# A decode block on one core: the last gate's weights carried by the last cache transfer, and one block of w2 brought in 26 five-row transfers

## Chip, core and metric

The kernel runs on one core of one Trainium2 chip. The metric is the device time of one execution in microseconds (us); lower is better. Before the change it is 1056.6 us, the median of three runs (1055.8 to 1057.46).

## What is computed

One token passes through an attention block with a long cache and then through a feed-forward block, both with modulated layer norms. All data is float32. Cut to what matters:

```
mod = silu(c) @ w_mod                 # c: 1 x 640, w_mod: 640 x 3840
sa, ca, ga, sb, cb, gb = six parts of mod, 640 each
h = layernorm(x) * (1 + ca) + sa
q = h @ wq                            # 32 heads of 192
o = softmax(q k^T / sqrt(192)) v      # k and v caches: 32 heads x 8192 x 192
x = x + ga * (o @ wo)                 # wo: 6144 x 640
h = layernorm(x) * (1 + cb) + sb
f = relu(h @ w1 + b1) ** 2            # w1: 640 x 1536
x = x + gb * (f @ w2 + b2)            # w2: 1536 x 640
```

The caches hold 403 MB, so nearly all of the work is bringing data in once.

## The kernel before

The data comes in as **transfers of about 8 MB** on one queue, that of SyncE (SP). They land in a ring of three slots, each 64.5 KB on every one of the 128 partitions (`slot`, L96; `load`, L197). `plan` (L50) cuts the caches into 53 chunks. A chunk holds some key positions, some units of values (eight positions each) and, in some chunks, a piece of wq ("q") or of wo ("o") at the end of each row ("mixed" transfers). Chunk 50 has the last keys, chunks 51 and 52 only values (nine and seven units), chunk 51 also the wo piece of pair 14. Chunk 52 comes in two pieces, of four and three units. After the chunks come three loads for the end, each into the next free slot: wm1 (the wo piece of the last pair 15 and the parts ga, sb, cb of w_mod), w1 (gb's part of w_mod, then w1 itself), and w2. They are cut at `WM_CUT`, `W1_CUT` and `W2_CUT` (L43 to L45), so that reading can begin before all has landed. wm1's first piece has the wo piece and the first three of five row blocks of the modulation weights. Load n+3 is issued by `load(n + 3)` at the end of step n (L401) and waits until chunk n has been read.

In the loop over chunks (L354 to L401) the values go to TensorE (`values`, L298, sums over positions with the softmax weights as stationary operand), the keys to VectorE (`multiply`, L249, by the query, and `scores`, L257, which sums over 192), with a part of the first addition on GpSimd (L376). `softmax` (L268) turns a head's scores into weights, `evict` (L303) brings a finished head back from PSUM and transposes it, `turn` (L318) scales it, `attend` (L324) multiplies a pair of heads by wo into `att_a`.

The order of work is written out by hand, and every engine works through its own instructions in that order. The order of the end on TensorE is: values of chunk 51, `attend(14)`, values of chunk 52, the transpose of the last evicted head, `attend(15)` (needs wm1's first piece), `mod(2, 3)` (L171; the three parts ga, sb, cb; its last two row blocks need wm1's second piece) with `gather` (L338) after the third of five row blocks, the two small sums of `layernorm` (L137), `gate(5)` (L183 to L192: twenty matmuls with gb's weights from w1's first piece, then four copies on ScalarE), the matmuls `pf` with w1 (L428), one idle matmul (L438), and the matmuls `py` with w2 (L446). `pf` needs `hT2`, the transposed result of the second layer norm (L422). Between `pf` and `py` VectorE makes `fT` (L431 to L434).

Two tiles that the change touches are held for the whole program: `qb` (L224), a ring of query rows that `query` fills and `multiply` reads, and `att_s` (L235), which is zeroed on VectorE early in the program and used only by `gather`.

Of the kernel before, what the change touches and what calls it, by code (L numbers as in the profile page):

```python
# [35 lines left out]
SRING = 4 * NPOS  # L36
WQ = KB * QC
UNIT = E * DH
SLOT = 84 * DH
VPC = 5  # L40
LEAD_FROM = 1300
LEAD = 120
W1_CUT = (KB * D + 3 * FF, KB * D + KB * FF)  # L43
W2_CUT = (8 * D, 11 * D, 12 * D)
WM_CUT = (WO + 9 * D, WO + 15 * D)  # L45
WARM = 1
EPS = 1e-5
# [2 lines left out]
def plan():  # L50

    chunks, kp, vp, q, o = [], 0, 0, 1, 0
    while kp < H * NPOS or vp < H * NPOS // E:
        room, w = SLOT, []
        if o < NPAIR - 1 and 2 * (o + 1) * NPOS // E <= vp:
            w.append(("o", o))
            o, room = o + 1, room - WO
        used = (QC * (q - 2) - 1) // DH + 1 if q > 2 else 0
        if q < NQ and kp >= NPOS * (QC * q // DH) - 3 * NPOS // 2 and kp >= NPOS * used:
            w.append(("q", q))  # L60
            q, room = q + 1, room - WQ
        if not chunks:
            nk, nv = NPOS, 0
        else:
            v = VPC - 1 if kp >= LEAD_FROM else VPC
            nk = min(H * NPOS - kp, (room - v * UNIT) // DH)
            if kp + nk - E * (vp + v) > LEAD:
                v += 1
                nk = min(H * NPOS - kp, (room - v * UNIT) // DH)
            nv = min(H * NPOS // E - vp, (room - nk * DH) // UNIT)  # L70
            while nv and ((vp + nv - 1) // (NPOS // E) + 1) * NPOS > kp + nk:
                nv -= 1
            nk = min(H * NPOS - kp, (room - nv * UNIT) // DH)
        chunks.append((kp, nk, vp, nv, w))
        kp, vp = kp + nk, vp + nv
    assert q == NQ and o == NPAIR - 1
    return chunks


def width(chunk):  # L80
    return chunk[1] * DH + chunk[3] * UNIT + sum(WO if t == "o" else WQ for t, _ in chunk[4])


PLAN = plan()


@with_exitstack
def block_kernel(ctx: ExitStack, tc: tile.TileContext, kv, wm0, wm1, w1, w2, out):
    nc = tc.nc
    const = ctx.enter_context(tc.tile_pool(name="const", bufs=1))  # L90
    strm = ctx.enter_context(tc.tile_pool(name="strm", bufs=3))
# [100 lines left out]
            nc.scalar.activation(mods[r, m], ps[r, DG * (g % 2):DG * (g % 2 + 1)], AF.Copy)  # L192

    chunk_t = {}
    start = [sum(width(c) for c in PLAN[:n]) * P for n in range(len(PLAN))]

    def load(n):  # L197
        if n < len(PLAN):
            chunk_t[n] = slot(f"chunk{n}")
            m = width(PLAN[n])  # L200
            cuts = (m,) if n + 1 < len(PLAN) else ((PLAN[n][3] + 1) // 2 * UNIT, m)
            pieces = [(kv[start[n]:start[n] + P * m].rearrange("(p n) -> p n", p=P), cuts)]
        else:
            name, src, cuts = (("wm1_t", wm1, WM_CUT), ("w1_t", w1, W1_CUT), ("w2_t", w2, W2_CUT))[n - len(PLAN)]
            chunk_t[name] = slot(name)
            n, pieces = name, [(src, cuts)]
        for src, cuts in pieces:
            a = 0
            for b in cuts:
                nc.sync.dma_start(chunk_t[n][:, a:b], src[:, a:b])  # L210
                a = b
# [9 lines left out]
        return ca1  # L221

    h1 = layernorm(x_c, 1, scale_a, lambda: ma[:, :KB, 0], "ln1")
    qb = const.tile([P, RING], F32, name="qb")  # L224

    def query(u, w):
        w = w.rearrange("p (b n) -> p b n", b=KB)
        ps = psum.tile([P, 512], F32, tag="q", name=f"ps_q{u}", bufs=2)
        for b in range(KB):
            nc.tensor.matmul(ps, h1[:, b:b + 1].to_broadcast([P, P]), w[:, b], start=(b == 0), stop=(b == KB - 1))  # L230
        nc.scalar.activation(qb[:, QC * u % RING:QC * u % RING + QC], ps, AF.Copy, scale=DH ** -0.5)  # L231


    att_a = psum.tile([P, 512], F32, tag="att", name="att_a")
    att_s = const.tile([P, D], F32, name="att_s")  # L235
    nc.vector.memset(att_s, 0.0)
    query(0, wm0_t[:, KB * 2 * D:KB * 2 * D + WQ])

    sc = const.tile([P, SRING], F32, name="sc")
# [63 lines left out]
    def evict(h):  # L303

        n = 32 * NV
        if h % 2 == 0:
            os_t["part"] = work.tile([P, 2, ED], F32, tag="os", name=f"os{h // 2}")
        os_ = os_t["part"]
        om = work.tile([P, ED, E], F32, tag="om", name=f"om{h}", bufs=1)
        nc.vector.tensor_mul(om[:n], ps_t.pop(h)[:n].rearrange("p (d e) -> p d e", e=E),  # L310
                             mask[:n, None, :].to_broadcast([n, ED, E]))
        nc.vector.tensor_reduce(os_[:n, h % 2], om[:n], axis=AX.X, op=ALU.add)  # L312
        if h % 2:
            i = h // 2
            os_t[i] = psum.tile([P, 512], F32, tag="sm", name=f"ps_oT{i}", bufs=2)
            nc.tensor.transpose(os_t[i][:, :n], os_[:n].rearrange("p a d -> p (a d)"), ident[:n, :n])  # L316

    def turn(i):  # L318
        oT = work.tile([P, NV], F32, tag="oT", name=f"oT{i}")
        nc.vector.tensor_reduce(oT, os_t[i][:, :96].rearrange("p (j r) -> p j r", j=NV), axis=AX.X, op=ALU.add)  # L320
        nc.vector.tensor_scalar(oT, oT, ri_t.pop(i), None, op0=ALU.mult)  # L321
        os_t[i] = oT
# [14 lines left out]

    def gather():  # L338

        nc.vector.tensor_copy(att_s[96:, :512], att_a[96:, :512])  # L340
        for j in range(NV):
            r = slice(32 * j, 32 * (j + 1))
            nc.scalar.activation(att_s[r, 512:], att_a[r, (D - 512) * j:(D - 512) * (j + 1)], AF.Copy)
        att_t.append(psum.tile([P, 512], F32, tag="o", name="att", bufs=3))
        for g in range(G):
            nc.tensor.matmul(att_t[0][32 * g:32 * (g + 1), :DG], sel.to_broadcast([P, 32]),
                             att_s[:, DG * g:DG * (g + 1)], start=True, stop=True)
# [6 lines left out]
    for n, (kp, nk, vp, nv, extra) in enumerate(PLAN):  # L354
        t = chunk_t.pop(n)
        kt = t[:, :nk * DH].rearrange("p (i d) -> p i d", d=DH) if nk else None
        vt = t[:, nk * DH:nk * DH + nv * UNIT].rearrange("p (j g n) -> p j g n", g=NV, n=E * ED) if nv else None
        at = nk * DH + nv * UNIT
        wo_t = None
        for what, k in extra:  # L360
            w = t[:, at:at + (WO if what == "o" else WQ)]
            at += w.shape[1]
            if what == "q":
                query(k, w)
            else:
                wo_t = (k, w)
        done = (kp + nk) // NPOS - 1 if nk and (kp + nk) // NPOS > kp // NPOS else None
        late = [v for v in range(vp, vp + nv) if v // (NPOS // E) not in p_t]
        for v in range(vp, vp + nv):
            if v not in late:  # L370
                values(vt[:, v - vp], v)
        if nk:
            multiply(kt, kp, nk)
            m = nk - POOL * nk // 16
            half = kt[:, m:, :DH // 2]
            nc.gpsimd.tensor_add(half, half, kt[:, m:, DH // 2:])  # L376
        if to_invert is not None:
            inverse(to_invert)
            to_invert = None
        evicted, to_evict = to_evict, []  # L380
        for h in evicted:
            evict(h)
        if nk:
            scores(kt[:, :m], kp)
        for h in evicted:
            if h % 2:
                turn(h // 2)
        if nk:
            scores(half, kp + m)
        if done is not None:  # L390
            softmax(done)
            if done % 2:
                to_invert = done // 2
        for v in late:
            values(vt[:, v - vp], v)
        for v in range(vp, vp + nv):
            if v % (NPOS // E) == NPOS // E - 1:
                to_evict.append(v // (NPOS // E))
        if wo_t is not None:
            attend(*wo_t)  # L400
        load(n + 3)  # L401

    wm1_t, w1_t, w2_t = chunk_t["wm1_t"], chunk_t["w1_t"], chunk_t["w2_t"]
    gb_t = w1_t[:, :KB * D].rearrange("p (b n) -> p b n", b=KB)
    w1_t = w1_t[:, KB * D:KB * (FF + D)].rearrange("p (b n) -> p b n", b=KB)
    w2_t = w2_t[:, :FB * D].rearrange("p (b n) -> p b n", b=FB)

    for h in to_evict:
        evict(h)
    turn(NPAIR - 1)  # L410
    attend(NPAIR - 1, wm1_t[:, :WO])
    mod(2, 3, wm1_t[:, WO:WO + KB * 3 * D].rearrange("p (b n) -> p b n", b=KB), gather)
# [8 lines left out]

    hT2 = columns(layernorm(x1, 32, scale_b, lambda: mods[:, 3], "ln2"), DG, "hT2")  # L422

    gate(5, gb_t)
    pf = psum.tile([P, 512], F32, tag="q", name="ps_f", bufs=2)
    for b in range(KB):
        for g in range(G):
# [15 lines left out]
    py = psum.tile([P, 512], F32, tag="q", name="ps_y", bufs=2)  # L443
    for b in range(FB):
        for g in range(G):
            nc.tensor.matmul(py[32 * g:32 * (g + 1), :DG], fT[:, b], w2_t[:, b, DG * g:DG * (g + 1)],  # L446
                             start=(b == 0), stop=(b == FB - 1))
    y = const.tile([P, DG], F32, name="y")
    nc.vector.tensor_mul(y, py[:, :DG], mods[:, 5])
# [44 lines left out]
```

## Time and profile before

| | |
|---|---|
| median of 3 runs | 1056.6 us |
| profiled execution, its own time | 1055.57 us |
| span of the profiled execution | 1053.8 us |
| VectorE busy | 830.2 us (79%) |
| TensorE busy | 495.8 us (47%) |
| moved by the DMA engines | 452.15 MB, 429 GB/s over the span |
| TensorE clock granted, mean | 0.713 |

A page of the profile lists busy time, transfers, the chain of work that ended last, and groups of instructions by line of the kernel (L298 is line 298). PE is TensorE, PEld its weight load, DVE VectorE, ACT ScalarE, POOL GpSimd, SP SyncE; SPq is SP's queue of transfers. Busy shares are averages over the whole span; what the end is worth is read from the timeline and the windows of the last 50 us.

### The profile page before, as it was taken

The page shows a single profiled execution, that of the slowest core. Times are in us where ns is not written, and L with a number is a line of the kernel's source. Part 1 is how long each engine was busy: PE and PEld are TensorE (multiplying, and loading weights), DVE is VectorE, ACT ScalarE, POOL GpSimd, SP SyncE. Part 2 cuts the span into 40 slices and gives each one's busy share as a digit, 9 for nine tenths or more (in the row PEclk, how much of TensorE's full clock was granted, in tenths as well). Part 3 has the DMA queues.
Part 4 walks back from the last instruction along what each step waited for, and adds up shares of the span by engine and source line. Part 5 has one row for each costly group of instructions (what it writes and reads, how often), then busy time and mean ns, then how long its engine had stood idle before and what let it go on. Part 6 is the DMA issues. An engine that isn't in the chain of part 4 may idle for free.

```text
span 1053.8 us, 5121 instructions
## 1 busy us (share of the span) xinstructions
PE 495.8 (47%) x2102; PEld 134.6 (13%) x2102; DVE 830.2 (79%) x428; ACT 43.4 (4%) x122; POOL 188.1 (18%) x57
## 2 busy tenths in 40 slices
PE   2153335455352363536344357344446346345286
PEld 1010011011010010101011011011011011011023
DVE  2898878877959969887797895999887977988822
ACT  1000000000000000000000000000000000000001
POOL 0212121121212202212121121122211211211200
PEclk9676576777675686668676577676777767768699
DMA  9999999999999999999999999999999999999997
GB/s 408 434 429 431 429 441 438 441 431 433 430 431 431 432 433 430 433 435 438 435 427 436 433 427 430 436 439 433 431 432 431 432 436 433 437 433 430 419 431 311
DMA packets 8959, 452.15 MB, mean 429 GB/s; under 512 B 996, under 2 KB 1000, under 8 KB 1256
## 3 DMA queue, kind: packets, MB, share of 16 engines
q1 hardware_dynamic: 8936, 451.83, 99.3%
q8 instruction: 16, 0.26, 0.1%
q14 instruction: 7, 0.06, 0.0%
HBM read 451.82 MB, written 0.00 MB: 429 GB/s over the span
## 4 chain that ended last, share of the span: by engine, by line
DMA 56%; DVE 31%; PE 11%; ACT 1%; issue 0%; SPq 0%; DVEq 0%
DMA chunk<-in_kv 53%; DVE chunk L249 16%; DVE sc L257 13%; PE ps_o L298 5%; DMA w_t<-in_w 2%; PE ps_q L230 2%; PE att_a L331 2%; DMA wm_t<-in_wm 1%; DVE os L312 1%; DVE om L310 1%; ACT p L281 0%; PE ps_mod L179 0%; PE ps_mx L273 0%; PE ps_mod L188 0%; PE att_a L333 0%
## 5 line engine op out<-in xcount | busy, mean ns | idle before, releaser
L249 DVE TENSOR_TENSOR chunk<-chunk,qb 128x8064 f32<-128x8064 f32 (+19 forms) x81 | 419.7, 5211 | 128.4 <-DMA chunk<-in_kv 123.2
L257 DVE TENSOR_REDUCE sc<-chunk 128x25 f32<-128x4800 f32 (+21 forms) x109 | 333.9, 3097 | 0.4
L298 PE MATMUL ps_o<-chunk,p 128*32 128x512 f32 x1536 | 296.7, 736 | 73.7 <-DMA chunk<-in_kv 64.3
L376 POOL TENSOR_TENSOR chunk<-chunk 128x1824 f32<-128x1824 f32 (+9 forms) x51 | 187.4, 3674 | 806.3 <-DVE chunk L249 548.4
L273 PE MATMUL ps_mx<-ident,mp 128*128 128x128 f32 x32 | 14.6, 455 | 343.9 <-DVE mp L271 343.9
L298 PEld LDWEIGHTS ps_o<-chunk,p 128*32 128x32 f32 x1536 | 67.4, 131 | 278.1 <-issue 188.1
L331 PE MATMUL att_a<-chunk,oT 128*32 128x512 f32 x90 | 63.4, 863 | 42.2 <-DVE oT L321 42.2
L230 PE MATMUL ps_q<-chunk,ln_h 128*128 128x512 f32 x110 | 66.9, 769 | 26.1 <-DMA chunk<-in_kv 26.1
L273 PEld LDWEIGHTS ps_mx<-ident,mp 128*128 128x128 f32 x32 | 5.6, 176 | 373.0 <-DVE mp L271 304.0
L281 ACT ACTIVATE p<-sc,nm 128x256 f32<-128x256 f32 x32 | 16.2, 507 | 649.9 <-DVE nm L275 649.9
L230 PEld LDWEIGHTS ps_q<-chunk,ln_h 128*128 128x128 f32 x110 | 26.5, 252 | 64.5 <-issue 35.1
L310 DVE TENSOR_TENSOR om<-ps_o,mask 96x512 f32<-96x512 f32 x32 | 21.6, 675 | 8.5 <-PE ps_o L298 8.5
L275 DVE TENSOR_REDUCE nm<-ps_mx 128x1 f32<-128x128 f32 x32 | 9.3, 292 | 19.5 <-PE ps_mx L273 19.5
L312 DVE TENSOR_REDUCE os<-om 96x64 f32<-96x512 f32 x32 | 21.8, 682 | 1.1
L331 PEld LDWEIGHTS att_a<-chunk,oT 128*32 128x32 f32 x90 | 11.7, 145 | 77.4 <-DVE oT L321 44.4
L320 DVE TENSOR_REDUCE oT<-ps_oT 128x3 f32<-128x96 f32 x16 | 4.0, 248 | 20.3 <-PE ps_oT L316 20.3
L286 PE MATMUL ps_sum<-ident,wide 128*128 128x128 f32 x16 | 7.5, 467 | 22.4 <-ACT wide L284 22.4
L179 PE MATMUL ps_mod<-wm_t,silu 128*32 128x320 f32 (+1 forms) x80 | 9.2, 608 | 15.5 <-DVE silu L167 15.5
L316 PE MATMUL ps_oT<-ident,os 96*128 96x96 f32 x16 | 5.0, 313 | 22.3 <-DVE os L312 22.3
L333 PE MATMUL att_a<-chunk,oW 128*96 128x384 f32 x30 | 14.1, 550 | 0.0
L231 ACT ACTIVATE qb<-ps_q 128x512 f32<-128x512 f32 x12 | 7.2, 597 | 136.7 <-PE ps_q L230 136.7
L329 ACT ACTIVATE oW<-oT 128x96 f32<-128x96 f32 x16 | 4.5, 280 | 177.5 <-DVE oT L321 177.5
(84 smaller groups left out, 100.9 us busy)
## 6 DMA issues: line engine op xcount, KB each, us to landing
chunk<-in_kv SPq DMA_DIRECT2D x38, 8064.0 KB, 37.5
chunk<-in_kv SPq DMA_DIRECT2D x11, 8000.0 KB, 38.3
chunk<-in_kv SPq DMA_DIRECT2D x2, 7872.0 KB, 38.5
chunk<-in_kv SPq DMA_DIRECT2D x1, 6144.0 KB, 27.6
wm_t<-in_wm SPq DMA_DIRECT2D x1, 4493.5 KB, 13.6
w_t<-in_w SPq DMA_DIRECT2D x1, 3904.0 KB, 20.7
wm_t<-in_wm SPq DMA_DIRECT2D x1, 3840.0 KB, 23.8
chunk<-in_kv SPq DMA_DIRECT2D x1, 3072.0 KB, 28.2
```

What stands on the lines that cost most here:

```text
L230: nc.tensor.matmul(ps, h1[:, b:b + 1].to_broadcast([P, P]), w[:, b], start=(b == 0), stop=(b == KB - 1))
L249: nc.vector.tensor_mul(pr, pr, q[:, None, :].to_broadcast([P, b - a, DH]))
L257: nc.vector.tensor_reduce(sc[:, a % SRING:a % SRING + b - a], src[:, a - first:b - first], axis=AX.X, op=ALU.add)
L273: nc.tensor.transpose(ps[:, :P], mp.to_broadcast([P, P]), ident)
L275: nc.vector.tensor_reduce(nm, ps[:, :P], axis=AX.X, op=ALU.max, negate=True)
L281: nc.scalar.activation(p, s[:, :, None].to_broadcast([P, NPOS, 32 // E]), AF.Exp, bias=nm, accum_out=sp[:, h % 2:h % 2 + 1])
L298: nc.tensor.matmul(ps_t[h][32 * g:32 * (g + 1)], p[:, E * j:E * (j + 1)].rearrange("p e r -> p (e r)"), t[:, g], start=(j == 0), stop=last)
L310: nc.vector.tensor_mul(om[:n], ps_t.pop(h)[:n].rearrange("p (d e) -> p d e", e=E), mask[:n, None, :].to_broadcast([n, ED, E]))
L312: nc.vector.tensor_reduce(os_[:n, h % 2], om[:n], axis=AX.X, op=ALU.add)
L331: nc.tensor.matmul(att_a[96:, :512], oT[:, j:j + 1].to_broadcast([P, 32]), w[:, j, :512], start=(first and j == 0), stop=(last and j == NV ...
L333: nc.tensor.matmul(att_a[:96, :NV * (D - 512)], oW.rearrange("p j r -> p (j r)"), w[:, :, 512:], start=first, stop=last)
L376: nc.gpsimd.tensor_add(half, half, kt[:, m:, DH // 2:])
```

## The change

The part of w_mod that makes gb moves from the head of the w1 load to the end of chunk 52's rows, in its second piece ("g" in the plan). `gate(5)` moves from after the second layer norm to right after the last `evict`, before `turn(15)` and `attend(15)`. Row block 0 of w2 leaves the w2 load. It gets an input array `w2x` and a tile `w2x_t` of its own, filled by 26 transfers: one after each `load(n + 3)` for n from 4 to 29, five rows of 640 floats each and three rows in the last. The w2 load keeps the other eleven blocks and is cut at new places; its last piece is now only the last 160 columns of the last block. `qb` and `att_s` now share one buffer: `att_s` is made in `gather`, and zeroed there on GpSimd.

```
+EXTRA = {"o": WO, "q": WQ, "g": KB * D}
-W1_CUT = (KB * D + 3 * FF, KB * D + KB * FF)
-W2_CUT = (8 * D, 11 * D, 12 * D)
+W1_CUT = (3 * FF, KB * FF)
+W2_CUT = (7 * D, 11 * D - DG, 11 * D)
+FEW = 5
+FEW_FROM = 4
...
+    chunks[-1][4].append(("g", 0))
...
+    w2x_t = const.tile([P, D], F32, name="w2x_t")
...
-    qb = const.tile([P, RING], F32, name="qb")
+    qb = work.tile([P, RING], F32, name="qb", tag="qb", bufs=1)
...
-    att_s = const.tile([P, D], F32, name="att_s")
-    nc.vector.memset(att_s, 0.0)
...
 def gather():
+        att_s = work.tile([P, D], F32, name="att_s", tag="qb", bufs=1)
+        nc.gpsimd.memset(att_s, 0.0)
...
         load(n + 3)
+        a = FEW * (n - FEW_FROM)
+        if 0 <= a < P:
+            b = min(a + FEW, P)
+            nc.sync.dma_start(w2x_t[a:b], w2x[a:b])
...
     for h in to_evict:
         evict(h)
+    gate(5, gb_t)
     turn(NPAIR - 1)
     attend(NPAIR - 1, wm1_t[:, :WO])
...
     hT2 = columns(layernorm(x1, 32, scale_b, lambda: mods[:, 3], "ln2"), DG, "hT2")
-    gate(5, gb_t)
     pf = psum.tile([P, 512], F32, tag="q", name="ps_f", bufs=2)
...
-            nc.tensor.matmul(py[...], fT[:, b], w2_t[:, b, ...],
+            nc.tensor.matmul(py[...], fT[:, b], (w2_t[:, b - 1] if b else w2x_t)[...],
```

Sizes: gb's weights are 1600 KB, one block of w2 is 320 KB, one row of it 2560 bytes. All bytes are still brought in once.

More of the change, by code (lines that the diff above doesn't have):

```diff
@@ L76, in plan, with block_kernel @@
     assert q == NQ and o == NPAIR - 1
+    chunks[-1][4].append(("g", 0))
     return chunks
 def width(chunk):
-    return chunk[1] * DH + chunk[3] * UNIT + sum(WO if t == "o" else WQ for t, _ in chunk[4])
+    return chunk[1] * DH + chunk[3] * UNIT + sum(EXTRA[t] for t, _ in chunk[4])
 PLAN = plan()
 @with_exitstack
-def block_kernel(ctx: ExitStack, tc: tile.TileContext, kv, wm0, wm1, w1, w2, out):
+def block_kernel(ctx: ExitStack, tc: tile.TileContext, kv, wm0, wm1, w1, w2, w2x, out):
     nc = tc.nc
@@ L358, in block_kernel @@
         at = nk * DH + nv * UNIT
-        wo_t = None
+        wo_t = gb_t = None
         for what, k in extra:
-            w = t[:, at:at + (WO if what == "o" else WQ)]
+            w = t[:, at:at + EXTRA[what]]
             at += w.shape[1]
@@ L364, in block_kernel @@
                 query(k, w)
+            elif what == "g":
+                gb_t = w.rearrange("p (b n) -> p b n", b=KB)
             else:
@@ L401, in block_kernel @@
         load(n + 3)
+        a = FEW * (n - FEW_FROM)
+        if 0 <= a < P:
+            b = min(a + FEW, P)
+            nc.sync.dma_start(w2x_t[a:b], w2x[a:b])
     wm1_t, w1_t, w2_t = chunk_t["wm1_t"], chunk_t["w1_t"], chunk_t["w2_t"]
-    gb_t = w1_t[:, :KB * D].rearrange("p (b n) -> p b n", b=KB)
-    w1_t = w1_t[:, KB * D:KB * (FF + D)].rearrange("p (b n) -> p b n", b=KB)
-    w2_t = w2_t[:, :FB * D].rearrange("p (b n) -> p b n", b=FB)
+    w1_t = w1_t[:, :KB * FF].rearrange("p (b n) -> p b n", b=KB)
+    w2_t = w2_t[:, :(FB - 1) * D].rearrange("p (b n) -> p b n", b=FB - 1)
     for h in to_evict:
         evict(h)
+    gate(5, gb_t)
     turn(NPAIR - 1)
@@ L445, in block_kernel @@
         for g in range(G):
-            nc.tensor.matmul(py[32 * g:32 * (g + 1), :DG], fT[:, b], w2_t[:, b, DG * g:DG * (g + 1)],
+            nc.tensor.matmul(py[32 * g:32 * (g + 1), :DG], fT[:, b], (w2_t[:, b - 1] if b else w2x_t)[:, DG * g:DG * (g + 1)],
                              start=(b == 0), stop=(b == FB - 1))
@@ L475 @@
     v = a(A_v_cache).reshape(H, P, NPOS // E, E, NV, ED).transpose(1, 0, 2, 4, 5, 3).reshape(P, H * NPOS // E, UNIT)
+    gb = rows(wm[:, 5 * D:], KB)[None]
     kv = [np.concatenate([k[:, kp:kp + nk].reshape(P, -1), v[:, vp:vp + nv].reshape(P, -1)]
-                         + [(wo if what == "o" else wq)[i] for what, i in extra], axis=1).reshape(-1)
+                         + [{"o": wo, "q": wq, "g": gb}[what][i] for what, i in extra], axis=1).reshape(-1)
           for kp, nk, vp, nv, extra in PLAN]
@@ L483 @@
         "wm1": np.concatenate([wo[-1], rows(wm[:, 2 * D:5 * D], KB)], axis=1),
-        "w1": np.concatenate([rows(wm[:, 5 * D:], KB), rows(B_w1, KB)], axis=1),
-        "w2": rows(B_w2, FB),
+        "w1": rows(B_w1, KB),
+        "w2": rows(B_w2, FB)[:, D:],
+        "w2x": rows(B_w2, FB)[:, :D],
     }
```

## The prediction

> **What bounds the kernel now.** I read the page first: the transfers and their rate, then the last part of the chain of waits.
>
> ```profile
> span 1053.8 us, 5121 instructions
> GB/s 408 434 429 431 429 441 438 441 431 433 430 431 431 432 433 430 433 435 438 435 427 436 433 427 430 436 439 433 431 432 431 432 436 433 437 433 430 419 431 311
> DMA packets 8959, 452.15 MB, mean 429 GB/s; under 512 B 996, under 2 KB 1000, under 8 KB 1256
> q8 instruction: 16, 0.26, 0.1%
> wm_t<-in_wm SPq DMA_DIRECT2D x1, 3840.0 KB, 23.8
> wm_t<-in_wm SPq DMA_DIRECT2D x1, 1920.0 KB, 28.1
> w_t<-in_w SPq DMA_DIRECT2D x1, 1536.0 KB, 24.0
> w_t<-in_w SPq DMA_DIRECT2D x1, 320.0 KB, 26.6
> ```
>
> Only the last slice (311 GB/s) falls away, so the transfers run back to back until a few us before the end. The change moves the same bytes, so no stage before the end gets shorter; the question is the last 50 us. Here is the chain in order of time, with columns start, us, what:
>
> ```profile
> 943.04 39.25 DMA chunk<-in_kv
> ...
> 1001.66 9.86 PE ps_o L298 x54
> ...
> 1015.98 20.69 DMA w_t<-in_w
> 1036.71 4.43 PE ps_mod L188 x20
> 1041.14 3.41 PE ps_f L428 x40
> ...
> 1046.98 3.50 PE ps_y L446 x96
> ```
>
> Chunk 50's landing, at 943.04 + 39.25 = 982.3, is the last one that the middle of the kernel waits for. The chain then names w1's first piece (landed at 1036.67) and the gate that follows it. But the page's chain follows only what came last. TensorE's timeline shows what runs beside it:
>
> ```profile
> 1015.88 6.21 PE L298 MATMUL ps_o<-chunk,p 128*32 128x512 f32 x42
> 1023.61 0.30 PE L316 MATMUL ps_oT<-ident,os 96*128 96x96 f32 x1 [1.52 <-DVE os L312]
> 1024.59 2.76 PE L331 MATMUL att_a<-wm_t,oT 128*32 128x512 f32 x6 [0.68 <-DVE oT L321]
> ...
> 1030.81 1.79 PE L179 MATMUL ps_mod<-wm_t,silu 128*32 128x480 f32 x16
> ...
> 1037.75 0.34 DVE L122 STREAM_TRANSPOSE hT<-ln_h 128x160 f32<-128x160 f32 x1
> ```
>
> From 1001.66 to the end of `mod(2, 3)` at 1032.60 TensorE has almost no gap, and the layer norm after it delivers hT2 at 1038.09, only 3.0 us before `pf` starts. So the gate can be worth 3.0 us at most, not 4.43.
>
> **The change, part by part. The gate.** It now sits between the transpose that ends at 1023.91 and `attend(15)`. How long it takes there depends on TensorE's clock, the column after POOL in the windows view (the next one is the mean DMA share):
>
> ```profile
> 1022.10:1024.60 2.50, 0.31 (x2) 0.15 (x2) 1.86 (x4) 0.03 (x1) 0.00 (x0) 1.00 1.03 439
> 1032.60:1036.40 3.80, 0.71 (x5) 0.59 (x4) 2.42 (x8) 0.06 (x1) 0.00 (x0) 1.00 0.96 410
> 1036.40:1039.81 3.41, 3.10 (x12) 1.48 (x14) 1.36 (x5) 0.20 (x1) 0.00 (x0) 0.50 1.09 458
> 1039.81:1044.40 4.59, 4.59 (x50) 1.62 (x46) 0.00 (x0) 1.18 (x4) 0.00 (x0) 1.00 0.97 410
> ```
>
> After 3.8 us in which TensorE worked 0.71 us, the clock was half for 3.41 us, and 3.10 us of the gate ran in that time. At full clock the gate is 3.10 / 2 + (1041.14 - 1039.81) = 1.55 + 1.33 = 2.9 us. At its new place the clock was 1.00, so it ends at 1023.91 + 2.9 = 1026.8. Its four ScalarE copies then stand ahead of `attend(15)`'s own copy (oW), but that is first needed 2.7 us after `attend(15)` begins, so I cost them at nothing.
>
> Behind the gate `attend(15)` waits: it needs wm1's first piece, and gb's 1600 KB now come ahead of that (1.638 MB / 429 GB/s = 3.8 us). The timeline of SP has the issue times:
>
> ```profile
> 998.97 0.81 SPq L210 DMA_DIRECT2D wm_t<-in_wm  x2
> 1015.98 7.44 SPq L210 DMA_DIRECT2D w_t<-in_w  x5
> ```
>
> The first piece lands at 998.97 + 23.8 + 3.8 = 1026.6, the second near 999.4 + 28.1 + 3.8 = 1031.3. `attend(15)` therefore starts at 1026.8 instead of 1024.59, **2.2 us later**, and everything to hT2 shifts with it: the last two blocks of `mod(2, 3)` run from 1033.0, after the second piece; hT2 is ready at 1040.3. w1's bytes end where they did, since what stands ahead of that point is the same sum: its second piece lands at 1016.4 + 24.0 = 1040.4, and `pf` needs it only for the last two of its five blocks. `pf` starts at 1040.35 instead of 1041.07: **0.7 us earlier**. Of the 4.43 us the gate gave up, 2.9 are paid again ahead of `attend(15)`.
>
> **pf's clock.** The gate was also what brought the clock back: `pf` ran at 1.00. Now TensorE is nearly idle from 1034.8 (1032.60 + 2.2) to 1040.35, 5.5 us, longer than the 4.1 us that lost the clock before. If `pf` then runs at half clock as long as the gate did (3.10 us), it gets 1.55 us longer. The bounds are 0 (the clock holds) and 3.4 us (all of `pf`'s 3.41 us at half clock); I take **+1.55**, from the nearest row. The Trainium skill, page "TensorE: Matmul & The Clock Gate", section "Part 1: The HAM clock gate (the "warmup" mystery)", says that an idle window of about 3.4 us halves the clock and about 3.4 us of work restores it; the rows above agree (3.41 us at 0.50). By its figure the term would be 1.7 us.
>
> The same clock adds a smaller term. The values of chunk 51 (9.86 us from 1001.66) began at half clock:
>
> ```profile
> 1002.27:1005.68 3.41, 3.41 (x15) 0.77 (x12) 1.19 (x2) 0.00 (x0) 0.00 (x0) 0.50 0.95 405
> ```
>
> That lasted to the end of this window, 4.0 us. The clock changes in whole steps of 3.41 us (from 1005.68 to 1036.40 are nine), and where they fall against the work is chance. 3.10 us of work in a step were enough above, so the slow stretch can last from 3.1 to 3.1 + 3.41 = 6.5 us, 4.8 in the middle. Before, up to 3.0 us of delay there was covered by the gate's wait; afterwards `attend(15)` has 0.2 us of cover. The middle length costs (4.8 - 4.0) / 2 - 0.2 = **0.2 us**, the longest 1.0.
>
> **The end of w2.** `py` follows `pf` by the same 2.4 us and so moves with it. Its last block begins 3.2 us after its start, near 1051, and w2's last piece landed near 1023.0 + 26.6 = 1049.6. A block less of w2 takes 0.75 us off that (0.328 MB / 429 GB/s), but `py` does not wait there, so the saving is worth **0**. The smaller last piece is worth nothing for the same reason.
>
> **The 26 transfers.** Their cost on an engine is read from the last rows of w2, which have the same 2560 bytes (the transfers of 1048.3 to 1049.0):
>
> ```profile
> DMA packets 27, 0.06 MB, mean 84 GB/s; under 512 B 4, under 2 KB 4, under 8 KB 27
> q1 hardware_dynamic: 27, 0.06, 21.5%
> ```
>
> 21.5% of 16 engines' 0.7 us is 2.41 us for 23 rows: 0.105 us each. A load writes a small completion packet for every engine that takes part: 62 loads x 16 + 4 = 996, the count under 512 B on the page. So the 62 loads of 128 rows used all 16 engines and the output of four rows used four; five rows will use five. The Trainium skill, page "DMA: Bandwidth & Descriptors", section "Why a DMA increments its semaphore by 16 and not by 1", says so too, and that these are always the lowest-numbered engines; the count agrees, the numbers of the engines no view here shows. If they are always the same five, each gets 26 x 0.105 = 2.7 us more. If they rotated, each of 16 would get 0.85 us, no more than the block of w2 that leaves its end.
>
> Whether 2.7 us on five engines cost anything depends on how evenly the sixteen run. The last column but one of these windows is the share of them at work:
>
> ```profile
> 1044.00:1045.00 1.00, 1.00 (x10) 0.30 (x2) 0.43 (x1) 0.00 (x0) 0.00 (x0) 1.00 0.91 376
> 1047.00:1048.00 1.00, 1.00 (x32) 1.00 (x36) 0.29 (x1) 0.00 (x0) 0.00 (x0) 1.00 0.48 197
> 1049.00:1050.00 1.00, 1.00 (x37) 1.00 (x32) 0.00 (x0) 0.00 (x0) 0.00 (x0) 1.00 0.01 3
> ```
>
> The engines finish between 1045 and about 1049, 4 us apart, and about half of them before 1047. An engine that is under 4 - 2.7 = 1.3 us behind the first has room; one at the tail makes every landing after it 2.7 us later. I take 0 and keep 2.7 as the other end. On SP an issue is 0.4 us (998.97, two in 0.81) and the loads around it are 37 us ahead of their landing, so nothing queued behind a small transfer is late.
>
> **The rest.** The zeroing of att_s cost 0.59 us on VectorE, where the first `multiply` waited 5.17 us for the query afterwards; on GpSimd it follows that engine's last addition and is needed 30 us later. Nothing either way, at most 0.6 us if it slowed the last scores.
>
> ```profile
> 24.11 0.59 DVE L236 MEMSET att_s<- 128x640 f32 x1
> ...
> 31.97 12.96 DVE L249 TENSOR_TENSOR chunk<-chunk,qb 128x12288 f32<-128x12288 f32 x1 [5.17 <-ACT qb L231]
> ```
>
> **Sum:** -0.7 + 1.55 + 0.2 = +1.05 us. The profiled execution took 1055.57 us, so it would take 1056.6; that execution is 1.0 us under the median of 1056.6, and against the median I get **1057.7 us**.
>
> **The rivals.** *The clock holds* through the 5.5 us, or returns after a moment: then -0.7 is all that is left, 1055.9 us. For it: the small sums of the layer norm run in the gap; against it: they ran in the 3.8 us above too.
>
> *The five engines are late ones.* This ends slower. Landings from chunk 50 on are 1.9 to 2.7 us later, 1059.6 to 1060.4 us. It decides as soon as one of the five is over 1.3 us behind the first. For it: half of the engines are; against it: only that the other half is not.
>
> *A small transfer costs more than its bytes.* Foreign packets do: the 16 instruction packets took 0.1% of 16 x 1053.8 us, 1.05 us each, for 16 KB that take 0.6 us at 27 GB/s. With 0.44 us more each, 26 cost 11 us more on five engines, about 1068 us. Against it: the rows of w2 above, in the loads' own queue, show no such gap.
>
> *The gate is hidden and the transfers set the end:* `pf` would start at 1038.1, and `py` would meet w2's last piece. That lands at 1049.6 - 0.75 = 1048.9, and with one of twelve blocks of `py` (0.3 us) behind it `py` ends at 1049.2 instead of 1050.48: 1.3 us less, 1055.3 us. Against it: `attend(15)` is behind the gate.
>
> **How the numbers follow.** Forecast 42%, clock holds 15%, late engines 28%, dear small transfers 8%, gate hidden 7%. 0.2% is 2.1 us, about what a measurement of this kernel can tell from no change. Slower by more: late engines, dear transfers and a tenth of the forecast, 40%. Faster by more: no case reaches it unless w2 lands earlier than I count, 5%. Within: 55%. The range runs from the clock that holds (1055.9) to the late engines with some of the clock's bound (1060.8); the dear transfers and the hidden gate stay outside. The forecast's own range is 1056.6 to 1058.7.
>
> **What would show it.** The gate at about 2.9 us with `attend(15)` right behind it near 1027; hT2 near 1040.3; a clock of 0.50 at the start of `pf`, which takes about 5 us. Were chunk 50 to land 2 us later than 982.3, late engines are the cause. A `pf` that starts before 1039.5 or `py` waiting for w2 would prove the sum wrong.

## The result and the profile after

| | before | after |
|---|---|---|
| median | 1056.37 us (6 runs, 1055.8 to 1057.46) | 1061.14 us (6 runs, 1060.45 to 1061.85) |
| ratio, 95% interval | 1 | 1.0042 [1.0032, 1.0053] |
| profiled execution | 1055.57 us | 1061.85 us |
| its span | 1053.8 us | 1060.1 us |

The change makes the kernel 4.8 us slower. The prediction said 1 us slower, and the time lies 0.3 us above its range. The page of the changed kernel first:

```profile
span 1060.1 us, 5151 instructions
GB/s 407 430 429 445 436 429 432 432 434 429 430 436 429 432 429 428 427 428 433 434 430 429 427 437 431 433 434 431 436 427 433 431 443 433 429 433 427 426 426 254
DMA packets 9216, 452.15 MB, mean 427 GB/s; under 512 B 1125, under 2 KB 1257, under 8 KB 1385
```

The bytes are the same. The packets under 512 B are 129 more than before: 128 of them are completion packets of the 26 transfers, one for each row (25 x 5 + 3), so within a transfer each row went to an engine of its own. The mean rate is 2 GB/s lower. The chain of waits, in order of time (start, us, what):

```profile
947.26 39.26 DMA chunk<-in_kv
986.54 8.56 DVE chunk L252
...
1003.20 27.61 DMA wm_t<-in_wm
```

Chunk 50 lands at 986.5 instead of 982.3: **4.2 us late**, before anything of the moved gate has run. TensorE's timeline of the end (start, us, line, what, in brackets the idle time before and what ended it):

```profile
1027.75 2.91 PE L192 MATMUL ps_mod<-chunk,silu 128*64 128x320 f32 x20
1030.95 2.73 PE L334 MATMUL att_a<-wm_t,oT 128*32 128x512 f32 x6 [0.29 <-DMA wm_t<-in_wm]
...
1037.14 1.79 PE L183 MATMUL ps_mod<-wm_t,silu 128*32 128x480 f32 x16
1044.53 6.24 PE L438 MATMUL ps_f<-w_t,hT 128*32 128x384 f32 x40 [1.89 <-issue]
1053.13 0.48 PE L456 MATMUL ps_y<-w2x_t,fT 128*32 128x160 f32 x8 [1.31 <-DVE fT L126]
```

The same matmuls `pf` before:

```profile
1041.07 3.43 PE L428 MATMUL ps_f<-w_t,hT 128*32 128x384 f32 x40
```

The gate takes 2.91 us, `attend(15)` follows it after a wait of 0.29 us for wm1's first piece, and `pf` starts 3.46 us later than the 1041.07 of before: the 4.2 us of chunk 50 less the 0.7 us that the prediction gave the gate. `pf` itself takes 6.24 us instead of 3.43, 2.8 us more. `py` waits for `fT`, not for w2. So the 6.3 us between the two spans are +4.2 (landings), -0.7 (gate) and +2.8 (`pf`); between the medians there are 4.8, since the profiled execution of before (1055.57 us) was faster than all six of its timed runs and that of after was its slowest.

The windows show the clock around `pf` (busy us of PE, PEld, DVE, ACT and POOL, then TensorE's clock, DMA share, GB/s):

```profile
1040.01:1043.43 3.42, 0.71 (x4) 0.59 (x4) 1.88 (x10) 0.26 (x1) 0.00 (x0) 1.00 1.03 433
1043.43:1046.84 3.41, 2.31 (x16) 0.90 (x20) 0.93 (x3) 0.00 (x0) 0.00 (x0) 0.50 0.97 411
1046.84:1050.25 3.41, 3.41 (x25) 1.12 (x20) 0.00 (x0) 0.00 (x0) 0.00 (x0) 0.50 0.71 293
```

As before the change, a stretch in which TensorE worked 0.71 us is followed by half clock. But `pf` began 1.1 us into the next step, worked 2.31 us of it, and did not get the clock back at its end; a second step at half clock followed, up to 1050.25.

Where do the 4.2 us come from? Windows over long stretches in the middle, of before and then of after:

```profile
200.00:400.00 200.00, 92.14 (x363) 24.15 (x362) 161.46 (x75) 7.05 (x21) 35.13 (x10) 0.71 1.00 433
400.00:600.00 200.00, 91.01 (x345) 23.45 (x345) 164.64 (x81) 6.57 (x20) 39.79 (x11) 0.67 1.00 433
700.00:900.00 200.00, 96.67 (x370) 26.17 (x368) 168.77 (x79) 7.68 (x23) 40.33 (x11) 0.72 1.00 433
```

```profile
200.00:400.00 200.00, 90.58 (x362) 23.72 (x362) 160.52 (x75) 7.06 (x21) 35.12 (x10) 0.72 1.00 431
400.00:600.00 200.00, 89.38 (x344) 23.12 (x344) 162.06 (x78) 6.57 (x20) 39.79 (x11) 0.69 1.00 430
700.00:900.00 200.00, 99.47 (x373) 26.37 (x371) 168.05 (x75) 7.69 (x23) 36.62 (x10) 0.72 1.00 433
```

The small transfers are issued after chunks 4 to 29, so they run from about 160 to 640 us. In the two windows that lie within it the rate is 2 to 3 GB/s lower although the DMA share is 1.00 as before; after 700 us it is 433 again. 2.5 of 433 GB/s over these 400 us are 2.3 us. A few more rows on five engines would not lower the rate of all of them together, so something else is lost there. On SP nothing waits for a small transfer:

```profile
169.37 0.34 SPq L215 DMA_DIRECT2D chunk<-in_kv  x1
169.75 0.32 SPq L412 DMA_DIRECT2D w2x_t<-in_w2x  x1
```

The packet records of the trace tell the two losses apart. Every engine writes its completion packet when its share of a load is done, so each load has sixteen such times. The first and the last of them, in us, and their distance (the spread), each from one profiled execution, with those of the experiments told below:

```
                     chunk 3: first  spread   chunk 50: first    last   spread
before                        84.36    2.33            977.75  981.87     4.12
after                         84.39    1.67            980.15  986.04     5.89
end only                      84.29    2.89            977.64  982.11     4.47
few only                      84.34    1.97            979.80  985.51     5.70
own five                      84.36    1.58            977.75  983.52     5.77
own three                     84.39    1.74            977.98  981.83     3.85
cross three                   84.38    1.91            979.74  983.46     3.72
sixteen rows                  84.36    1.70            981.55  986.07     4.52
kept clock                    84.44    2.88            977.79  982.27     4.47
own four                      84.49    1.71            977.84  983.67     5.84
foreign three                 84.33    3.19            980.05  984.66     4.62
```

At chunk 3, ahead of the small transfers, before and after agree. At chunk 50 the first engine of after is 2.4 us late and the last 4.2: **2.4 us that every engine loses and 1.8 us that the last one loses on top.** A load needs all sixteen, so the last counts. One execution is enough to tell such times apart: in the six kernels of the table in which no row lands in another engine's partitions the first engine ends chunk 50 between 977.6 and 978.0, in the other five between 979.7 and 981.6.

### The profile page after: what moved, and what is told of

Read it like the earlier page. It is cut to its first block, busy times and chain, and to the rows that moved or that the text cites. A ratio compares the mean times of both kernels' runs of the same rounds, so it can differ in the third digit from the quotient of the medians.

```text
span 1060.1 us, 5151 instructions
## 1 busy us (share of the span) xinstructions
PE 492.1 (46%) x2102; PEld 133.4 (13%) x2102; DVE 829.6 (78%) x427; ACT 43.5 (4%) x122; POOL 188.6 (18%) x58
## 4 chain that ended last, share of the span: by engine, by line
DMA 57%; DVE 31%; PE 10%; ACT 1%; issue 1%; SPq 0%; DVEq 0%
DMA chunk<-in_kv 53%; DVE chunk L252 16%; DVE sc L260 13%; DMA wm_t<-in_wm 4%; PE ps_o L301 4%; PE att_a L334 2%; PE ps_q L235 2%; PE ps_mod L183 1%; PE ps_f L438 1%; DVE os L315 1%; DVE om L313 1%; PE ps_mx L276 0%; ACT p L284 0%; PE att_a L336 0%; PE ps_y L456 0%
## 5 line engine op out<-in xcount | busy, mean ns | idle before, releaser
L235 PE MATMUL ps_q<-chunk,ln_h 128*128 128x512 f32 x110 | 63.3, 733 | 25.9 <-DMA chunk<-in_kv 25.9
```

## The experiments

Theory: the 26 transfers cost 4 us in two ways. (a) One of the five engines that carry them was late already and becomes the last of all. (b) A row that its engine writes into partitions which another engine serves in the large loads holds all sixteen up for a moment. The rivals: the end (the gate's place and `pf`'s clock) costs it; or a small transfer costs the same wherever its rows go. The lines shown of an edit are against the changed kernel unless the text starts from another one. All ratios are against the kernel before, run beside it on the same chip, with 95% intervals; "lands" is the start of VectorE's multiply of chunk 50.

**End only.** The change without the 26 transfers; w2 whole again.

```
-W2_CUT = (7 * D, 11 * D - DG, 11 * D)
+W2_CUT = (8 * D, 12 * D - DG, 12 * D)
...
-            nc.sync.dma_start(w2x_t[a:b], w2x[a:b])
```

> The end of the change alone: gb in chunk 52, the gate ahead of attend(15), the shared buffer; no five-row transfers, w2 whole in its own load with a last piece of 160 columns. Theory: the 26 small transfers made chunk 50 land 4.2 us late, the end itself costs little. Then chunk 50 lands at 982.3 us as before, attend(15) starts near 1026.8, pf starts near 1040.4 and runs 5 to 6.3 us at half clock: 1057.2 to 1058.5 us. Rival (the late landing comes from the end's edits, such as the shared buffer of qb and att_s or the longer last chunk): chunk 50 lands near 986.5 and the time is near 1061.

Measured: 1057.14 us, ratio 1.0010 [1.0001, 1.0019]. Chain and then TensorE's timeline:

```profile
943.33 39.24 DMA chunk<-in_kv
982.60 8.56 DVE chunk L251
```

```profile
1023.43 2.91 PE L192 MATMUL ps_mod<-chunk,silu 128*64 128x320 f32 x20
1026.99 2.73 PE L333 MATMUL att_a<-wm_t,oT 128*32 128x512 f32 x6 [0.65 <-DMA wm_t<-in_wm]
...
1040.57 5.87 PE L433 MATMUL ps_f<-w_t,hT 128*32 128x384 f32 x40 [1.89 <-issue]
```

The end alone costs 1.1 us of the 4.8, about what the prediction's sum for it was (+1.05). `pf` starts 0.5 us earlier than before although chunk 50 landed 0.3 us later, and takes 2.4 us longer. The remaining 3.7 us of the change belong to the transfers.

**Few only.** The other half alone: the 26 transfers, gate and gb's weights where they were.

```
-W1_CUT = (3 * FF, KB * FF)
-W2_CUT = (7 * D, 11 * D - DG, 11 * D)
+W1_CUT = (KB * D + 3 * FF, KB * D + KB * FF)
+W2_CUT = (7 * D, 10 * D, 11 * D)
...
-    gate(5, gb_t)
     turn(NPAIR - 1)
...
+    gate(5, gb_t)
     pf = psum.tile([P, 512], F32, tag="q", name="ps_f", bufs=2)
```

> The 26 transfers alone, one block of w2 in a tile of its own; gate and gb where they were before. Theory: chunk 50 and w1's first piece land 4.2 us later (near 986.5 and 1040.9), the gate and pf run as before behind them: 1060.6 us. Rival (the small transfers cost nothing beyond their bytes): landing 982.3, about 1056.4 us.

Measured: 1059.94 us, ratio 1.0038 [1.0026, 1.0051]. The chain:

```profile
946.72 39.26 DMA chunk<-in_kv
986.01 8.56 DVE chunk L251
```

The transfers alone make chunk 50 3.7 us late and the kernel 3.9 us slower. With the 1.1 us of the end alone that makes 5.0, and the whole change costs 4.8: the two halves add up.

**Own five.** End only, with 26 five-row transfers into the change's tile, which nothing reads here (w2 is loaded whole as well, so 0.33 MB more are moved). The rows of one transfer are now every fourth partition, 0, 4, 8, 12, 16 and so on, so that each is written by the engine that serves it in the large loads.

```
+        k = n - FEW_FROM
+        if 0 <= k < 26:
+            a = k % 4 + 32 * (k // 4 % 2)
+            nc.sync.dma_start(w2x_t[a:a + 17:4], w2x[a:a + 17:4])
```

> The end as in the first run with w2 whole, and beside it 26 five-row transfers into a tile that nothing reads, their five rows four partitions apart (partitions 0 to 16 or 32 to 48 in steps of four), so that if row j goes by engine j, each engine writes only partitions that it also serves in the large loads. 0.33 MB more are brought in than in the changed kernel. Theory: the stall of all engines, 2.2 us in sum, comes from rows that one engine writes into partitions of another; it is gone, and 1.8 us remain because one of the five engines was the latest already: chunk 50 lands near 984.2, time 1.8 us over the first run. Rival (a price of each transfer, wherever its rows go): chunk 50 lands near 986.5, time near 1061.

**Own three.** The same with three rows: `w2x_t[a:a + 9:4]`.

> As the run with five rows, but three rows in each of the 26 transfers, again four partitions apart. Theory: three engines take part and the latest one is not among them; nothing is left of the 4.2 us, chunk 50 lands at 982.3 to 982.8 and the time is that of the first run. Rival (a price of each transfer for all engines): chunk 50 lands 2.2 us late, near 984.6, and the time is 2.2 us over the first run.

**Cross three.** Three rows again, but neighbours as in the change: `a = 5 * k if k < 25 else 125` and `w2x_t[a:a + 3]`.

> As the run with three rows four partitions apart, but the three rows of a transfer are neighbouring partitions (5k, 5k+1, 5k+2), as in the changed kernel, so that the engines write into partitions that another engine serves. Bytes, transfers and engines are the same. Theory (the stall of all engines comes from such rows): about three fifths of 2.2 us come back, chunk 50 lands near 983.6 (983.2 to 984.5) and the time is 0.9 to 2.2 us over that run, near 1058.8. Rival (three rows were harmless because they are few): chunk 50 lands at 982.3, 1057.5 us.

Measured: own five 1058.94 us, 1.0029 [1.0018, 1.0041]; own three 1057.53 us, 1.0012 [1.0003, 1.0021]; cross three 1058.89 us, 1.0025 [1.0016, 1.0034]. For each of them, in this order, the chain at chunk 50 and a window of the middle:

```profile
984.02 8.56 DVE chunk L252
```

```profile
200.00:400.00 200.00, 91.35 (x361) 23.86 (x360) 161.27 (x75) 7.08 (x21) 35.15 (x10) 0.71 1.00 433
```

```profile
982.32 8.56 DVE chunk L252
```

```profile
200.00:400.00 200.00, 90.48 (x360) 23.76 (x360) 161.45 (x75) 7.07 (x21) 35.15 (x10) 0.72 1.00 433
```

```profile
983.95 8.56 DVE chunk L252
```

```profile
200.00:400.00 200.00, 89.62 (x363) 23.89 (x362) 161.62 (x75) 7.06 (x21) 35.14 (x10) 0.71 1.00 431
```

The three split the loss. Own three costs nothing at chunk 50: 26 transfers are issued and completed as in the other two, and it lands at 982.32 as before. So neither a transfer's issue nor a fixed cost of it is what is paid. Own five adds 1.7 us, all of it in the spread (5.77 instead of 3.85), with the rate still at 433: one of the engines that carry rows four and five becomes the last, which is (a). Cross three adds 1.6 us with the spread unchanged (3.72) and the first engine 1.8 us late, the rate at 431: all sixteen are held up, which is (b). The Trainium skill, page "DMA: Bandwidth & Descriptors", section "The descriptor swizzle", gives the engine of a 128-partition load as 8 * (partition >> 6) + ((partition >> 2) & 7), which puts four neighbouring partitions on one engine; the rows of own five and own three were chosen by that, and the runs agree with it. What a row in another engine's partitions costs, the section does not say.

**Own four.** Own three with a fourth row, `w2x_t[a:a + 13:4]`: which engine is the late one?

> As the run with three rows four partitions apart, with a fourth row (partition 12 or 44 and so on). Theory: the fourth engine is the one that the instruction fetches had already made late, so all of the 1.7 us of the five-row run comes back with this one row: chunk 50 lands near 984.0, time near 1058.9 us. Rival (each further engine adds its share): half of it, 983.2 and 1058.2 us.

**Foreign three.** Own three with every partition moved on by 16, so that the same three engines write partitions that others serve. One number changes:

```
-            a = k % 4 + 32 * (k // 4 % 2)
+            a = 16 + k % 4 + 32 * (k // 4 % 2)
```

> The run with three rows four partitions apart with one number changed: the rows begin 16 partitions higher (16, 20, 24 and so on), so each goes into a partition that another engine (the fifth to seventh) serves in the large loads. Theory (foreign partitions stall all engines): chunk 50 lands 0.9 to 2.2 us late, 983.2 to 984.5, time 1058.4 to 1059.7 us. Rival (neighbouring rows were the reason in the run before, not whose partitions they are): 982.3 and 1057.5 us.

Measured: own four 1059.18 us, 1.0027 [1.0017, 1.0037]; foreign three 1059.67 us, 1.0030 [1.0019, 1.0042]. The chain of own four, then the chain and two windows of foreign three:

```profile
944.90 39.26 DMA chunk<-in_kv
984.19 8.56 DVE chunk L252
```

```profile
945.88 39.25 DMA chunk<-in_kv
985.15 8.56 DVE chunk L252
```

```profile
200.00:400.00 200.00, 91.84 (x364) 24.14 (x362) 159.74 (x75) 7.06 (x21) 35.13 (x10) 0.72 1.00 431
400.00:600.00 200.00, 88.84 (x344) 23.09 (x344) 164.24 (x79) 6.57 (x20) 39.78 (x11) 0.70 1.00 430
```

Own four has the whole of own five's loss: the spread is 5.84 us instead of 3.85, with the first engine where it was (977.84). It is the fourth row's engine that is late, and the packet records of before say how late: an engine that ends chunk 50 at 980.78, 3.0 us after the first, has 1.1 us of room to the last (981.87), and 26 rows of 0.105 us are 2.7. Foreign three differs from own three in where the rows go (the rows of w2x that are read move along), and the first engine is 2.1 us later. It landed 2.8 us after own three, more than was expected of it, as its spread is 0.8 us wider too. Part of that may have been there before any small transfer (3.19 at chunk 3).

The packet records also show the stall itself. Each large packet (one partition's 64000 or 64512 bytes) takes about 2.36 or 2.38 us. Of some 4000 that ran between 100 and 700 us, so many took over 2.42 us:

```
before           12        after            348
own three        17        few only         328
own four         16        cross three      296
own five         13        foreign three    370
                           sixteen rows     210
```

Around a transfer into foreign partitions, large packets on 12 to 16 of the sixteen engines (the mean of each kernel) are lengthened by over 15 ns; around one into own partitions it is none, or 0.2 in own three. So (b) is seen, not only inferred from the landing: rows in foreign partitions hold up packets that other engines are writing. In foreign three, three engines that carry none of the rows lose some 1.5 us more than the others; that they are the three whose partitions are written is likely and not shown.

**Sixteen rows.** The change with 8 transfers of 16 rows in place of 26: all engines get the same share, so (a) should go and (b) stay.

```
-FEW = 5
+FEW = 16
```

> The changed kernel with 8 transfers of 16 neighbouring rows in place of 26 of five; w2's first block is used as there. Each engine gets one row of each, so no engine is put behind the others and the 1.8 us of the late engine go; each gets 8 x 0.105 = 0.84 us in the middle. Theory (the stall counts rows in foreign partitions, 128 as before): 2.2 us of stall, chunk 50 lands near 985.4, about 1060 us. Rival (the stall counts transfers, 8 in place of 26): 0.7 us, chunk 50 lands near 983.8, about 1058.6 us.

Measured: 1060.77 us, 1.0044 [1.0031, 1.0056]; the chain:

```profile
946.94 39.55 DMA chunk<-in_kv
986.52 8.56 DVE chunk L252
```

The late engine is gone (spread 4.52), but every engine is 3.8 us late. Its own eight rows are 8 x 0.105 = 0.84 us of that; the other 3.0 us are the stall, more than the 2.2 us that I had expected. So an even spread over the engines saves nothing here.

**Kept clock.** End only, with five matmuls of 128 x 512 whose result nothing uses in the gaps of the second layer norm, to hold the clock up to `pf`.

```
+    def gap(k):
+        for _ in range((2, 1, 2)[k]):
+            nc.tensor.matmul(kept, ones, wm1_t[:, :512], start=True, stop=True)
```

> The end of the change alone, with five idle matmuls of 128 x 512 in the gaps of the second layer norm (two, one and two), whose result nothing reads, so that TensorE does not rest before pf. Theory: pf takes 3.4 us again, and the time falls by 1.2 to 2.4 us against the first run, to about 1055.5. Rival (pf is long because it waits for w1): pf stays at 5 to 6 us and the time at 1057.1.

Measured: 1056.35 us, 1.0004 [0.9995, 1.0013]. TensorE's timeline:

```profile
1040.60 3.43 PE L442 MATMUL ps_f<-w_t,hT 128*32 128x384 f32 x40
...
1047.01 2.38 PE L460 MATMUL ps_y<-w_t,fT 128*32 128x160 f32 x64 [1.92 <-DMA w_t<-in_w]
1049.83 1.29 PE L460 MATMUL ps_y<-w_t,fT 128*32 128x160 f32 x32 [0.44 <-DMA w_t<-in_w]
```

`pf` takes 3.43 us again, 2.4 less than in end only, so the clock was the whole of its loss. The time falls only by 0.8 us (1057.14 to 1056.35), less than the 1.2 to 2.4 expected: `py` now waits for w2, whose last blocks are in at 1049.8.

**Split gate.** The kernel before, with the gate's five row blocks in the three gaps of the layer norm (three, one, one) instead of behind it. The gate then costs no time of its own and keeps the clock. w1's first piece is cut after gb, w2 in four.

```
+    def gap(k):
+        gate(5, gb_t, pg, ((0, 1, 2), (3,), (4,))[k])
```

> The kernel before with the gate's five blocks of matmuls put into the three gaps of the second layer norm (three, one, one), gb's weights as a first piece of their own in w1's load, and w2 cut after 5, 9 and 12 blocks less 160 columns. No five-row transfers. Theory: the gate costs nothing there and keeps the clock; pf starts at hT2 near 1038.2 and ends near 1041.8, and then py waits for w2: the end is set by the landing of w2's last pieces, 0.5 to 0.9 us earlier than before, about 1055.3 us. Rival (the small sums of the layer norm are delayed by the gate's matmuls): hT2 comes over 1 us later and the time is 1056 or more.

Measured: 1056.26 us, 0.9999 [0.9990, 1.0007]. TensorE's timeline:

```profile
1037.48 2.14 PE L438 MATMUL ps_f<-w_t,hT 128*32 128x384 f32 x24 [1.21 <-DVE hT L122]
1040.78 1.50 PE L438 MATMUL ps_f<-w_t,hT 128*32 128x384 f32 x16 [1.16 <-DMA w_t<-in_w]
...
1047.70 1.29 PE L456 MATMUL ps_y<-w_t,fT 128*32 128x160 f32 x32 [1.38 <-DMA w_t<-in_w]
1049.85 1.02 PE L456 MATMUL ps_y<-w_t,fT 128*32 128x160 f32 x24 [0.86 <-DMA w_t<-in_w]
```

`pf` starts 3.6 us earlier than before (0.5 of them from chunk 50, which landed at 981.8), at full clock, and nothing is gained: it waits 1.16 us for w1, and `py` waits twice for w2, the last time until 1049.85. The landing of w2 that was expected 0.5 to 0.9 us earlier did not come. The 3.0 us that the prediction called the most the gate can be worth were there to be had at `pf`'s start, but not at the end. Neither of the two versions beats the kernel before by more than the measurement can tell.

## Why the prediction was wrong, point by point

- **The gate** (-0.7): right. 2.91 us against 2.9. What `attend(15)` waits for last was a near thing in the prediction (the gate's end at 1026.8, wm1's first piece at 1026.6), and in end only and the changed kernel it is wm1, by 0.65 and 0.29 us; in end only `attend(15)` at 1026.99 against 1026.8 and `pf` at 1040.57 against 1040.35; in the changed kernel `pf` at 1044.53, which is 1040.35 and the 4.2 us of chunk 50.
- **pf's clock** (+1.55, bounds 0 and 3.4): right in kind, too small in size. In end only it was +2.4, in the changed kernel +2.8. The step took `pf` at half clock "as long as the gate did", 3.10 us. The clock changes at fixed steps of 3.41 us, and whether the first one brings it back depends on how much of it `pf` fills: 2.31 us were not enough in the windows above. In own five, own three and own four `pf` took 4.9, 4.9 and 5.1 us, close to the forecast's 5: it ran 2.9 to 3.4 us at half clock (twice what it took beyond 3.43), about one step. So the size was chance, between +1.5 and +2.8. The estimate worked out from the Trainium skill's page "TensorE: Matmul & The Clock Gate", section "Part 1: The HAM clock gate (the "warmup" mystery)", 1.7 us, is met by the second kind of run (1.5 to 1.7) and not by the first (2.4 and 2.8). With the clock kept, only 0.8 us came back at the end, since w2 is next in line.
- **The values of chunk 51** (+0.2): their size as one term was not measured alone. From chunk 50's landing to the gate's place there were 41.6 us before (1023.91 - 982.32); in the changed kernel and in end only 41.2 and 40.8, in own five and own four 41.9 and 42.2. This scatters by as much as the prediction's bounds.
- **The end of w2** (0): right for the changed kernel, where `py` waits for `fT`. Kept clock and split gate show the limit that stands 0.8 us below end only.
- **The 26 transfers** ("I take 0 and keep 2.7 as the other end"): **this is the step that failed.** They cost 3.7 us (4.8 less the 1.1 of end only), and 3.9 tried alone. Two things were wrong in it. First, one of the five engines, the fourth, has less room than 2.7 us. Own three, own four and own five show it, 982.3, 984.2 and 984.0 us at chunk 50. The rival *the five engines are late ones* was thus true, at 1.7 to 1.9 us; it had 28%, which was too little by the step's own count: it put half of the engines out of room (at chunk 50 of before the packet records show nine of sixteen over 1.4 us behind the first), and with eight of sixteen, five taken blindly are all early in 1 case of 78. Second, the step counted bytes on the engines that carry them and nothing for the others. The stall of all sixteen, 2.4 us in the changed kernel, is no term of the sum and no rival; cross three and foreign three show it against own three, and so do the lengthened packets. It has the sign of the rival *a small transfer costs more than its bytes*, but its place is another: own three's transfers cost nothing, so it isn't the transfer, it is where its rows go.
- **SP's queue** ("nothing queued behind a small transfer is late"): right, an issue took 0.32 us.
- **The rest** (0): `att_s` and `qb` were not tried alone. They are within end only's 1.1 us, which the gate and `pf`'s clock already fill.

The prediction's own test, "were chunk 50 to land 2 us later than 982.3, late engines are the cause", would have misled: it landed 4.2 us later, and less than half of that is the late engine. Only the first engine's time beside the last one's tells the two apart.

Open: why rows in foreign partitions hold up all engines (the runs show that they do, and by how much), and why the fourth engine is late. In the packet records an engine's packets follow each other within a few ns, so each engine can be traced through the run. In before, one engine is put back about 1 us by each of three instruction fetches of 8 KB (at 101, 416 and 740 us) and is 3 us behind the first at chunk 50. In own four, the engine that has three such fetches (at 104, 425 and 741 us) carries a row of each of the 26 transfers and is the last at chunk 50 (983.67), and in own three no engine that carries rows has them. So this is the fourth engine; that the fetches are the whole cause is likely, but no run took them away.

## What to carry to other kernels

When transfers run back to back on all engines, a small transfer put among them is paid in full where an engine that carries it is already among the last and, if its rows go to partitions that other engines serve, by all engines; count it by rows and by where they land, not by its bytes. Look at how far apart the engines finish before giving any of them more, and lay rows that must be added so that each engine writes the partitions that it writes anyway. And before a step of the end is made shorter, find the next landing behind it: here the 3 us that split gate gained at `pf`'s start were worth nothing, since w2 arrives when it does.

## What the runs showed of the hardware that I had not expected

- Rows of 2560 bytes that land in other engines' partitions (as nearly all rows of these kernels do) cost all sixteen engines time together, measured at the first engine of chunk 50: 2.4 us for 128 rows (after), 2.0 for 78 (cross three, 979.74 - 977.75), 2.3 for 78 (foreign three) and 3.0 for 128 (sixteen rows), 0.02 to 0.03 us a row in each. In their own partitions 78 and 104 rows cost the first engine 0.2 and 0.1 us (own three, own four).
- The engines do not even out. Each runs its own share without a gap, and what puts one back stays: the spread grew from 2.3 us at chunk 3 to 4.1 at chunk 50 of before.
- TensorE's clock did not come back after a step of 3.41 us in which it worked 2.31 us (68%), and did after one with 3.10 us (91%).
